# A chunked GLU after attention: down projections gathered in SBUF for plain chunks, and projection reads moved to the sync engine's queue

## The chip, the core and the metric

The kernel runs on one core of a Trainium2 chip. A core has a matrix engine (TensorE; PE in the profile, and PEld for its loading of weights), a vector engine (DVE), a scalar engine (ACT), a general engine (GpSimd, POOL) and a sync engine (SP), which issues transfers. Each works through its own list of instructions in order. Transfers (DMAs) are issued from the lists of SP, ACT or POOL and carried out by 16 DMA engines. The metric is the time on the device in microseconds.

## What is computed

The reference takes 2048 tokens of 576 numbers and runs one transformer layer in float32:

- a layer norm, a projection to queries, keys and values, attention with 32 heads of 18 numbers in which each token sees itself and 7 earlier tokens at a distance of 2, an output projection `wo`, and the sum with the input: `h = x + attention(layernorm(x))`
- a layer norm of `h`, and a gated linear unit with 4608 hidden columns: `h + (sigmoid(n @ w_gate) * (n @ w_up)) @ w_down`, where `n` is the normalised `h`.

The result, 2048 x 576 numbers, goes back to DRAM.

## The kernel before

**Tiles.** The tokens are four blocks of 512, numbered 0 to 3: even and odd tokens, first and second half. The hidden columns are 36 chunks of 128. Every matmul operand is split into a high part in TensorE's float32r form and a low part, the remainder (`split`, line 103: one ACT copy and one DVE subtraction), and a product is three matmuls: high by high, low by high, high by low.

**Stages.** After a first part (queries, keys, values for all blocks, the attention of block 0), a list of work items runs, lines 877 and 878: 14 *plain* chunks (`std`, function `single`) of block 0, then 22 *paired* chunks (`pair`) of blocks 0 and 1, then 14 plain chunks of block 1, and 36 paired chunks of blocks 2 and 3. A paired chunk computes gate and up products of two blocks with seven products in place of eight. So there are two plain stages, and they run a single block's products each.

**Weights.** At item `c` the loop (line 1003) splits the weights of item `c + 1` (`weights`, line 509) and issues the load of item `c + 2` (`load_gu`, line 501, on SP's queue): a tile `wg` of 128 x 1856 numbers with gate, up and down columns, in two buffers. A load waits until the weights two items earlier are split, and the last of those splits waits for a matmul, since the tile `w4` has one buffer.

**Down projection.** The hidden tiles of two chunks make one unit of down projection, `down_units` (line 643). It goes through four groups of 128 tokens; each takes 12 matmuls into a PSUM tile `dp` (two buffers), and ACT copies the result to a tile `stage` in SBUF (line 668; the pool `st`, line 494, has two buffers of it). After the fourth group, POOL issues a DMA that adds `stage` to an accumulator in DRAM, `hacc` of the block (line 672). After the last unit of a block, `hacc` is copied to the output. In the last stage most pairs of chunks go another way (`down_seven`), and four chunks at the end add on DVE to a tile `tail` (line 670).

**Background.** Between the products a generator does other work in small steps (`bg_step`; eight steps in a plain chunk): under the first plain and paired chunks, the rest of the attention of block 1, its output projection and layer norm (`proj_scr`, line 721) and the operands of the paired stage; later the attention of blocks 2 and 3, and under the second plain stage their projections and the operands for the last stage. `proj_scr` first reads, on POOL's queue, four tiles `oj` of attention output from DRAM, four tiles `hj` of the input, and the split weights `wow` (line 727 and line 758), then waits some steps, and then takes four token groups through `proj_j`: transposes of `oj`, matmuls with `wo`, addition to `hj`, layer norm, transposes. Each `hj` is written out by POOL (lines 742 and 745). After the projections a `stage` tile is set to zero by POOL (line 833), and ACT's queue writes it to DRAM as the start of sums for the last stage.

**Order.** The program is written out by hand, item by item, but a planner orders each engine's list: an instruction is placed when its inputs and buffers are ready in the planner's own model of time, and by priority (`tc.high_priority`) among those that are ready. On the chip each list is then kept in that order.

Of the kernel before, what the change touches and what calls it, by code (L numbers as in the profile page):

```python
# [29 lines left out]
NF = F // P  # L30
NS = 4
# [3 lines left out]
DX = D + DR  # L35
# [8 lines left out]
BLOCKS = [(0, 0), (0, 1), (1, 0), (1, 1)]  # L44
# [3 lines left out]
DH2 = D // 2  # L48
# [5 lines left out]
HC = 700  # L54
NSTD = 14
NPL = 4
# [4 lines left out]
def kernel(ctx, tc, x, wqkv, wo, wmlp, out):  # L61
    nc = tc.nc
    dve, act, pool, pe, sp = nc.vector, nc.scalar, nc.gpsimd, nc.tensor, nc.sync
# [11 lines left out]
    xv = x.rearrange("(h p j e) d -> e h p j d", e=2, h=2, j=NS)  # L75
    ov = out.rearrange("(h p j e) d -> e h p j d", e=2, h=2, j=NS)
# [21 lines left out]
    def f32(ap):  # L98
        return ap.bitcast(F32)
# [125 lines left out]
            live = [gn for gn in live if next(gn, END) is not END]  # L225


    def proj_j(bank, oj, hj, wos, th, tl, xn_tile, put, order=(0, 1)):
        pv = tr_main(bank(), oj)
        with tc.high_priority(HI):  # L230
            split(th[:, 0:4], tl, pv)
        yield
        pv = tr_rest(bank(), oj)
        with tc.high_priority(HI):
            split_rest(th[:, 4], pv)
        yield
        for i in order:
            ps = bank()
            tok_major(ps, DH2, th, tl, slice(0, P), *wos[i])
            hs = hj[:, i * DH2:(i + 1) * DH2]  # L240
            with tc.high_priority(HI):
                dve.tensor_tensor(hs, hs, ps[:, :DH2], ALU.add)
            yield
        xn = xn_tile()
        with tc.high_priority(HI):
            ln_j(hj, xn, False)
# [122 lines left out]
    o = None  # L369
# [63 lines left out]
    h = load_x(0)  # L433
# [10 lines left out]
    def front():  # L444
        ar = tok_tile((P, 5, TB))
        oT = th_tile(), tl_tile()
        gens = []
        for j in range(NS):
            js = slice(j * P, (j + 1) * P)

            def put(pv, cs, js=js):
                act.activation(ar[:, cs, js], pv, AF.Copy)

            gens.append(proj_j(any_bank, o[:, j], h[:, j], wos, oT[0][:, :, js], oT[1][:, :, js],
                               lambda j=j: o[:, j], put, (1, 0)))
# [181 lines left out]
        between(6)  # L637

    tails = {}
    segs = [0] * 4  # L640
    NSEG = NF // 2

    def down_units(seg, b, t):
        e, hf = BLOCKS[b]
        left = NSEG - 1 - segs[b]
        segs[b] += 1
        add = b < 2 or left > 1
        if add:
            hs = st.tile([P, NS, D], F32, name="stage")
        else:  # L650
            hs = tails[b]
        for j in range(NS):
            js = slice(j * P, (j + 1) * P)
            ps = gp.tile([P, 2, 512], F32, bufs=2, name="dp")
            k = 0
            n = 3 * len(seg) - 1
            for hid, d in seg:
                hh, hl = hid[t]
                for a, m in ((hh, 0), (hl, 0), (hh, 1)):
                    for i in range(2):  # L660
                        pe.matmul(ps[:, i, :DH2], a[:, js], d[:, m, i * DH2:(i + 1) * DH2],  # L661
                                  start=k == 0, stop=k == n)
                    k += 1
            hv = hs[:, j].rearrange("p (i n) -> p i n", i=2) if add else \
                hs[:, :, j // 2, (j % 2) * DH2:(j % 2 + 1) * DH2]
            with tc.high_priority(HC):
                if add:
                    act.activation(hv, ps[:, :, :DH2], AF.Copy)  # L668
                else:
                    dve.tensor_tensor(hv, hv, ps[:, :, :DH2], ALU.add)  # L670
            if add and j == NS - 1:
                pool.dma_start(hacc[b], hs, accum_op=ALU.add, max_dma_last_dim=8 * D)  # L672
                if left == 0:
                    pool.dma_start(ov[e, hf], hacc[b])
            elif not add and left == 0:
                sp.dma_start(ov[e, hf][:, j].rearrange("p (i n) -> p i n", i=2), hv)
            yield

# [39 lines left out]
            sp.dma_start(f32(ww[a]), wscr[1][:, a])  # L718
        return tuple(ww)

    def proj_scr(pj, b, raw, wos, wait, at=0):
        e, hf = BLOCKS[b]
        th, tl = th_tile(), tl_tile()

        def load(shape, name, src):
            t = pj.tile([P, shape], F32, bufs=NS, name=name)
            pool.dma_start(t, src)
            return t

        def tile_j(j, oj, hj):  # L730
            js = slice(j * P, (j + 1) * P)
            xj = []

            def put(pv, cs):
                if raw is None and not xj:
                    xj.append(pj.tile([P, 5, P], F32, bufs=2, name="xj"))
                act.activation(xj[0][:, cs] if raw is None else raw[:, cs, js], pv, AF.Copy)

            yield from proj_j(bg_bank, oj, hj, wos,
                              th[:, :, js], tl[:, :, js], lambda: oj, put, (1, 0))  # L740
            if b < 2:
                pool.dma_start(hacc[b][:, j], hj)
            else:
                rows = slice(0, 7, 6) if b == 2 else slice(2, 5, 2)
                pool.dma_start(hsev[:, j // 2, rows, j % 2],
                               hj.rearrange("p (i n) -> p i n", i=2))
            if raw is None:
                act.dma_start(xscr[b][:, :, js], xj[0])

        ojs, hjs = [], []  # L750
        for j in range(NS):
            ojs.append(load(DX, "oj", oscr[b][:, j]))
            yield
        for j in range(NS):
            hjs.append(load(D, "hj", xv[e, hf][:, j]))
            if wos[0] is None and j == 0:
                ww = pj.tile([P, 2, 5, DH2], F32R, name="wow")
                pool.dma_start(f32(ww), wscr[0])
                wos[0] = ww[:, 0], ww[:, 1]
            yield  # L760
        for _ in range(wait):
            yield
        while c < at:
            yield
        live = [tile_j(j, ojs[j], hjs[j]) for j in range(NS)]
        for _ in range(5):
            for gn in live:
                next(gn)
                yield
        for gn in live:  # L770
            yield from gn
        if raw is not None:
            act.dma_start(xscr[b][:, 0:2], raw[:, 0:2])

    def operands(pp, p, Xn, names, own):
        def load(t):
# [21 lines left out]
    def under_first():  # L798
        wos = [None, wos_early()]
        for _ in ag:  # L800
            yield ATT
        at_stk.close()
        a1 = xt.tile([P, 5, TB], F32, tag="th", bufs=3, name="ar")
        with sb_pool("pj", "right") as pj:
            yield from proj_scr(pj, 1, a1, wos, 4, 6)
        with sb_pool("pp", "right") as pp:
            yield from operands(pp, 0, X, ("s2", "s3", "s1", "a11", "s4"), a1)

# [4 lines left out]
    def under_rest(last_x):  # L813
# [13 lines left out]
            wos[1] = wos_early()  # L827
        with sb_pool("pj2", "right") as pj:
            a0 = xt.tile([P, 5, TB], F32, tag="th", bufs=3, name="ar")
            yield from proj_scr(pj, 2, a0, wos, 4)  # L830
            yield from proj_scr(pj, 3, None, wos, 0)
        z = st.tile([P, NS, D], F32, name="stage")
        pool.memset(z, 0.0)
        for u in range(2):
# [168 lines left out]
    for c, (kind, p, f) in enumerate(items):  # L1003
# [37 lines left out]
        else:  # L1041
# [14 lines left out]
            if f < NF - NPL:  # L1056
                if f % 2:
                    if f == 1:
                        queue.append(lag(LAG))
                    queue.append(seven())  # L1060
                    for b in blocks:
                        segs[b] += 1
                continue
            d = M[f]
        seg.append((hid, d))
        if len(seg) == 2:
            if by_seven and not tails:
                tails.update({2: None, 3: None})
# [48 lines left out]
```

## Time and profile before

| | us |
|---|---|
| median of 3 runs | 1668.56 (1667.79 to 1675.57) |
| the profiled execution | 1668.82 |
| its span, first to last instruction | 1667.0 |
| PE busy | 1579.7 (95%) |
| DVE busy | 1248.2 (75%) |
| ACT busy | 897.9 (54%) |
| POOL busy | 215.5 (13%) |

The stages in the profile, by the sigmoids of the plain chunks: the first plain stage runs from about 260 to 427 us, the paired chunks of blocks 0 and 1 follow until about 815, the second plain stage until about 1022, and the rest is the paired stage of blocks 2 and 3. "Busy" of PE counts pipelined matmuls, so it says when PE was not idle, not how fast it ran; the granted clock beside it says that. A wait is written "engine line tile <- engine line tile": who stood idle, and whose end let it go on.

### The profile page before, as it was taken

To read this page: it belongs to the slowest core of one execution; us is meant where nothing else is said; L and a number is where in the kernel's file an instruction comes from. 1 tells how busy PE (TensorE), PEld (TensorE's weight loads), DVE (VectorE), ACT (ScalarE), POOL (GpSimd) and SP (SyncE) were. 2 spreads that over 40 slices of the span, in tenths; PEclk is the share of its full clock that TensorE was granted. 3 is DMA by queue.
4 is the path that set the end of the run, shared out by engine and by line. 5 is a ranking of instruction groups with operands and counts; after the bars stand their busy time and mean duration, and the time that the engine had idled before them with its cause. 6 is when DMAs were issued, how large, how long until landed. Compare 5 with 4: busy or idle time off the path is not lost.

```text
span 1667.0 us, 22497 instructions
## 1 busy us (share of the span) xinstructions
PE 1579.7 (95%) x8532; PEld 1396.4 (84%) x8532; DVE 1248.2 (75%) x1954; ACT 897.9 (54%) x1583; POOL 215.5 (13%) x266
## 2 busy tenths in 40 slices
PE   7899877899999999999998988999999999999998
PEld 6799776788788888888897877788888888888887
DVE  7999999447799999999454446677776777667755
ACT  5422224426555656655434244677766777667761
POOL 2000010210000100000211200122122121221210
PEclk9999988999999999999999999999999999999999
DMA  7446534737557576575956366589888898888983
GB/s 252 158 162 229 213 143 165 233 112 236 144 151 184 149 178 169 131 190 145 290 156 191 103 203 151 148 164 192 173 174 172 166 190 173 174 171 171 189 172 109
DMA packets 81341, 290.82 MB, mean 174 GB/s; under 512 B 8560, under 2 KB 17008, under 8 KB 80208
## 3 DMA queue, kind: packets, MB, share of 16 engines
q0 software_dynamic: 33616, 133.31, 40.3%
q1 hardware_dynamic: 36416, 132.33, 24.5%
q10 hardware_dynamic: 11200, 23.73, 3.8%
q8 instruction: 67, 1.10, 0.3%
q14 instruction: 42, 0.34, 0.1%
HBM read 147.19 MB, written 144.51 MB: 175 GB/s over the span
## 4 chain that ended last, share of the span: by engine, by line
PE 72%; DVE 12%; DMA 9%; ACT 3%; issue 2%; POOL 0%; SPq 0%; ACTq 0%; DVEq 0%; POOLq 0%
PE b L543 37%; PE dp L661 12%; PE dp L694 11%; PE b L550 7%; DMA wg<-in_wmlp_dram 6%; PE acc L150 2%; DVE pr L198 2%; DVE pr L172 1%; DVE lg L175 1%; PE b L150 1%; PE bgp L150 1%; DVE pr L203 1%; DVE w L105 1%; DVE tl L105 1%; DMA h<-stage 1%
## 5 line engine op out<-in xcount | busy, mean ns | idle before, releaser
L543 PE MATMUL b<-tl,w 128*128 128x512 f32 x1728 | 446.5, 399 | 17.1 <-DVE w L105 7.7
L543 PEld LDWEIGHTS b<-tl,w 128*128 128x128 f32 x1728 | 315.4, 190 | 78.2 <-DVE w L105 8.4
L543 PE MATMUL b<-th,w 128*128 128x512 f32 x1380 | 361.1, 397 | 6.0 <-DVE s L563 3.0
L543 PEld LDWEIGHTS b<-th,w 128*128 128x128 f32 x1380 | 252.5, 189 | 60.3 <-DVE s L625 4.6
L105 DVE TENSOR_TENSOR w<-wg,w 128x384 fp32r<-128x384 f32 (+2 forms) x200 | 129.0, 649 | 107.3 <-ACT w L104 107.0
L104 ACT ACTIVATE w<-wg 128x384 fp32r<-128x384 f32 (+2 forms) x200 | 117.9, 595 | 115.4 <-DMA wg<-in_wmlp_dram 72.1
L550 PE MATMUL b<-th,w 128*128 128x512 f32 x576 | 178.8, 392 | 0.0
L703 POOL DMA_DIRECT2D h<-ev x128 | 110.4, 863 | 459.6 <-ACT ev L700 444.7
L700 ACT ACTIVATE ev<-dp 128x576 f32<-128x576 f32 x224 | 145.0, 647 | 33.3 <-PE dp L694 30.5
L150 PE MATMUL acc<-qw,th 128*128 128x432 f32 x512 | 156.0, 365 | 0.0
L105 DVE TENSOR_TENSOR w<-tw,w 128x512 fp32r<-128x512 f32 x116 | 79.6, 686 | 72.8 <-ACT w L104 72.1
L668 ACT ACTIVATE stage<-dp 128x576 f32<-128x576 f32 x144 | 92.5, 645 | 70.8 <-PE dp L661 69.5
L661 PE MATMUL dp<-d,h1h 128*128 128x288 f32 x640 | 122.6, 302 | 7.6 <-ACT h1h L104 6.7
L550 PEld LDWEIGHTS b<-th,w 128*128 128x128 f32 x576 | 109.1, 189 | 23.1
L661 PE MATMUL dp<-d,h0h 128*128 128x288 f32 x640 | 121.4, 300 | 2.0 <-ACT stage L668 2.0
L104 ACT ACTIVATE w<-tw 128x512 fp32r<-128x512 f32 x116 | 73.2, 631 | 83.5 <-PE b L543 78.5
L661 PEld LDWEIGHTS dp<-d,h1h 128*128 128x128 f32 x640 | 101.3, 194 | 11.3 <-ACT h1h L104 7.2
L661 PEld LDWEIGHTS dp<-d,h0h 128*128 128x128 f32 x640 | 101.4, 193 | 5.7 <-ACT stage L668 2.3
L150 PEld LDWEIGHTS acc<-qw,th 128*128 128x128 f32 x512 | 98.3, 192 | 4.6 <-ACT th L104 0.3
L672 POOL DMA_DIRECT2D h<-stage x36 | 43.5, 1208 | 440.4 <-ACT stage L668 409.1
L150 PE MATMUL acc<-qw,tl 128*128 128x432 f32 x256 | 93.4, 365 | 0.0
L172 DVE TENSOR_TENSOR pr<-kw,q 128x1152 f32<-128x1152 f32 x64 | 85.2, 1354 | 4.7 <-DMA kw<-k 4.1
(272 smaller groups left out, 2890.6 us busy)
## 6 DMA issues: line engine op xcount, KB each, us to landing
h<-ev POOLq DMA_DIRECT2D x96, 576.0 KB, 6.9
wg<-in_wmlp_dram SPq DMA_DIRECT2D x48, 928.0 KB, 5.9
h<-stage POOLq DMA_DIRECT2D x36, 1152.0 KB, 11.5
wg<-in_wmlp_dram SPq DMA_DIRECT2D x36, 640.0 KB, 4.7
kw<-k SPq DMA_DIRECT2D x16, 792.0 KB, 4.2
vw<-v SPq DMA_DIRECT2D x16, 792.0 KB, 4.8
wd<-in_wmlp_dram SPq DMA_DIRECT2D x18, 576.0 KB, 7.0
h<-ev POOLq DMA_DIRECT2D x32, 288.0 KB, 6.2
```

The costliest lines, as they stand in the source:

```text
L104: act.activation(hi, src, AF.Copy)
L105: splits.append(dve.tensor_tensor(lo, src, f32(hi), ALU.subtract))
L150: pe.matmul(ps[:, :n], a[:, c, js], m[:, c], start=k == 0, stop=False)
L172: dve.tensor_tensor(pr[:, i], kw[:, j:j + W], q[:, j].unsqueeze(1).broadcast_to([P, W, CG]), ALU.mult)
L543: pe.matmul(ps, wt[:, a, k0 + c], xx[:, m + c], start=first and k == 0, stop=k == 5, skip_group_check=True)
L550: pe.matmul(ps, wt[:, a, k0], xx[:, 4], start=False, stop=a == 1, skip_group_check=True)
L661: pe.matmul(ps[:, i, :DH2], a[:, js], d[:, m, i * DH2:(i + 1) * DH2], start=k == 0, stop=k == n)
L668: act.activation(hv, ps[:, :, :DH2], AF.Copy)
L672: pool.dma_start(hacc[b], hs, accum_op=ALU.add, max_dma_last_dim=8 * D)
L694: pe.matmul(ps[:, i, :DH2], a[x][:, js], m[y], start=k in (0, 1, 3) and q == 0, stop=q == 2, skip_group_check=True)
L700: act.activation(hs[:, k % 2], ps[:, :, :DH2], AF.Copy)
L703: pool.dma_start(hsev[:, u, k0:k + 1], hs[:, :k + 1 - k0], accum_op=ALU.add, max_dma_last_dim=8 * D)
```

## The change

Three things are changed, and one function is split up.

1. **Down projection of plain chunks.** `down_units` becomes a tile of matmuls (`down_tile`), an eviction (`add_tile`) and an accumulating DMA (`add_dram`), from which three functions are put together. For plain chunks, `down_std` takes one `stage` tile for all 7 units of a block: the first unit is copied to it by ACT, the six others are added to it by DVE, and one accumulating DMA is sent after the seventh. For paired chunks of blocks 0 and 1, `down_units` is as before; for the end of the last stage, `down_tail` is as before.
2. **Reads of the background projections.** `oj`, `hj` and `wow` are read on SP's queue. Two steps of the background are between two reads of `oj`; the `hj` tiles and `wow` are read during the first steps of the token groups. The reads for block 3 are issued as the token groups of block 2 end. The waiting steps go; the projection of block 1 starts its reads at item 5, where its token groups had waited for item 6.
3. **Write-out of `hj`.** POOL's DMA is issued when the layer norm is done and the first transpose's result is to be copied, not at the end of the token group.

```diff
-    def down_units(seg, b, t):
...
+    def add_tile(hv, ps, copy):
+        with tc.high_priority(HC):
+            if copy:
+                act.activation(hv, ps, AF.Copy)
+            else:
+                dve.tensor_tensor(hv, hv, ps, ALU.add)
...
+    def add_dram(b, hs):
+        pool.dma_start(hacc[b], hs, accum_op=ALU.add, max_dma_last_dim=8 * D)
+        segs[b] += 1
+        if segs[b] == 1 + (NF - NSTD) // 2:
+            e, hf = BLOCKS[b]
+            pool.dma_start(ov[e, hf], hacc[b])
...
+    def down_std(seg, b, n):
+        if n == 0:
+            tails[b] = st.tile([P, NS, D], F32, name="stage")
+        hs = tails[b]
+        for j in range(NS):
+            add_tile(halved(hs, j), down_tile(seg, b, j), n == 0)
+            if j == NS - 1 and n == NSTD // 2 - 1:
+                add_dram(b, hs)
+            yield
...
+    def load_j(pj, b, j, i):
+        e, hf = BLOCKS[b]
+        t = pj.tile([P, D if i else DX], F32, bufs=NS, name="hj" if i else "oj")
+        sp.dma_start(t, (xv[e, hf] if i else oscr[b])[:, j])
+        return t
...
             def put(pv, cs):
-                if raw is None and not xj:
-                    xj.append(pj.tile([P, 5, P], F32, bufs=2, name="xj"))
+                if cs.start == 0:
+                    if b < 2:
+                        pool.dma_start(hacc[b][:, j], t[1])
...
-        ojs, hjs = [], []
-        for j in range(NS):
-            ojs.append(load(DX, "oj", oscr[b][:, j]))
-            yield
-        for j in range(NS):
-            hjs.append(load(D, "hj", xv[e, hf][:, j]))
...
-        for _ in range(wait):
-            yield
-        while c < at:
-            yield
...
+        todo = []
+        if ins is None:
+            ins = []
+            for j in range(NS):
+                ins.append([load_j(pj, b, j, 0), None])
+                yield
+                yield
+            todo = [0, 1, None, 2, 3]
+        live = [tile_j(t, j) for j, t in enumerate(ins)]
+        n = 0
         for _ in range(5):
             for gn in live:
+                if todo and n % 2 == 0:
+                    j = todo.pop(0)
+                    if j is not None:
+                        ins[j][1] = load_j(pj, b, j, 1)
+                    elif wos[0] is None:
+                        ww = pj.tile([P, 2, 5, DH2], F32R, name="wow")
+                        sp.dma_start(f32(ww), wscr[0])
+                        wos[0] = ww[:, 0], ww[:, 1]
+                n += 1
                 next(gn)
                 yield
-        for gn in live:
+        nxt = []
+        for j, gn in enumerate(live):
             yield from gn
+            if after is not None:
+                nxt.append([load_j(pj, after, j, i) for i in range(2)])
...
-            yield from proj_scr(pj, 1, a1, wos, 4, 6)
+            while c < 5:
+                yield
+            yield from proj_scr(pj, 1, a1, wos)
...
-            yield from proj_scr(pj, 2, a0, wos, 4)
-            yield from proj_scr(pj, 3, None, wos, 0)
+            ins = yield from proj_scr(pj, 2, a0, wos, after=3)
+            yield from proj_scr(pj, 3, None, wos, ins)
...
             for b in blocks:
-                queue.append(down_units(seg, b, b % 2))
+                queue.append(down_std(seg, b, f // 2) if kind == "std" else
+                             down_tail(seg, b, f == NF - 1) if by_seven else down_units(seg, b))
```

More of the change, by code (lines that the diff above doesn't have):

```diff
@@ L225, in run, with proj_j @@
             live = [gn for gn in live if next(gn, END) is not END]
-    def proj_j(bank, oj, hj, wos, th, tl, xn_tile, put, order=(0, 1)):
+    def proj_j(bank, t, wos, th, tl, xn_tile, put, order=(0, 1)):
+        oj = t[0]
         pv = tr_main(bank(), oj)
@@ L239, in proj_j @@
             tok_major(ps, DH2, th, tl, slice(0, P), *wos[i])
-            hs = hj[:, i * DH2:(i + 1) * DH2]
+            hs = t[1][:, i * DH2:(i + 1) * DH2]
             with tc.high_priority(HI):
@@ L245, in proj_j @@
         with tc.high_priority(HI):
-            ln_j(hj, xn, False)
+            ln_j(t[1], xn, False)
         yield
@@ L452, in put @@
                 act.activation(ar[:, cs, js], pv, AF.Copy)
-            gens.append(proj_j(any_bank, o[:, j], h[:, j], wos, oT[0][:, :, js], oT[1][:, :, js],
+            gens.append(proj_j(any_bank, (o[:, j], h[:, j]), wos, oT[0][:, :, js], oT[1][:, :, js],
                                lambda j=j: o[:, j], put, (1, 0)))
@@ L639 @@
     tails = {}
-    segs = [0] * 4
-    NSEG = NF // 2
-    def down_units(seg, b, t):
-        e, hf = BLOCKS[b]
[L645 to L651, printed above, removed]
-        for j in range(NS):
[L653 to L675, printed above, removed]
@@ new lines, with down_tile @@
+    segs = [0] * 2
+    def down_tile(seg, t, j):
+        js = slice(j * P, (j + 1) * P)
+        ps = gp.tile([P, 2, 512], F32, bufs=2, name="dp")
+        k = 0
+        n = 3 * len(seg) - 1
+        for hid, d in seg:
+            hh, hl = hid[t]
+            for a, m in ((hh, 0), (hl, 0), (hh, 1)):
+                for i in range(2):
+                    pe.matmul(ps[:, i, :DH2], a[:, js], d[:, m, i * DH2:(i + 1) * DH2],
+                              start=k == 0, stop=k == n)
+                k += 1
+        return ps[:, :, :DH2]
@@ new lines, in add_tile, with halved @@
+    def add_tile(hv, ps, copy):
[4 more added lines that the diff above has]
+                dve.tensor_tensor(hv, hv, ps, ALU.add)
+    def halved(hs, j):
+        return hs[:, j].rearrange("p (i n) -> p i n", i=2)
+    def add_dram(b, hs):
[4 more added lines that the diff above has]
+            pool.dma_start(ov[e, hf], hacc[b])
@@ new lines, in down_units @@
+    def down_units(seg, b):
+        hs = st.tile([P, NS, D], F32, name="stage")
+        for j in range(NS):
+            add_tile(halved(hs, j), down_tile(seg, b, j), True)
+            if j == NS - 1:
+                add_dram(b, hs)
[7 more added lines that the diff above has]
+            if j == NS - 1 and n == NSTD // 2 - 1:
+                add_dram(b, hs)
+            yield
@@ L676, in down_units, with down_tail @@
+    def down_tail(seg, b, end):
+        e, hf = BLOCKS[b]
+        hs = tails[b]
+        for j in range(NS):
+            hv = hs[:, :, j // 2, (j % 2) * DH2:(j % 2 + 1) * DH2]
+            add_tile(hv, down_tile(seg, b - 2, j), False)
+            if end:
                 sp.dma_start(ov[e, hf][:, j].rearrange("p (i n) -> p i n", i=2), hv)
@@ L719, in wos_early, with proj_scr, tile_j @@
         return tuple(ww)
-    def proj_scr(pj, b, raw, wos, wait, at=0):
+    def load_j(pj, b, j, i):
[3 more added lines that the diff above has]
+        return t
+    def proj_scr(pj, b, raw, wos, ins=None, after=None):
         e, hf = BLOCKS[b]
         th, tl = th_tile(), tl_tile()
[L725 to L730, printed above, removed]
+        def tile_j(t, j):
             js = slice(j * P, (j + 1) * P)
@@ L734, in put @@
             def put(pv, cs):
-                if raw is None and not xj:
-                    xj.append(pj.tile([P, 5, P], F32, bufs=2, name="xj"))
[L737 to L746, printed above, removed]
+                if cs.start == 0:
+                    if b < 2:
+                        pool.dma_start(hacc[b][:, j], t[1])
+                    else:
+                        rows = slice(0, 7, 6) if b == 2 else slice(2, 5, 2)
+                        pool.dma_start(hsev[:, j // 2, rows, j % 2],
+                                       t[1].rearrange("p (i n) -> p i n", i=2))
+                    if raw is None:
+                        xj.append(pj.tile([P, 5, P], F32, bufs=2, name="xj"))
@@ L747, in tile_j @@
+                act.activation(xj[0][:, cs] if raw is None else raw[:, cs, js], pv, AF.Copy)
+            yield from proj_j(bg_bank, t, wos, th[:, :, js], tl[:, :, js], lambda: t[0], put, (1, 0))
             if raw is None:
                 act.dma_start(xscr[b][:, :, js], xj[0])
-        ojs, hjs = [], []
-        for j in range(NS):
-            ojs.append(load(DX, "oj", oscr[b][:, j]))
-            yield
-        for j in range(NS):
-            hjs.append(load(D, "hj", xv[e, hf][:, j]))
[L756 to L759, printed above, removed]
-            yield
@@ L761, in proj_scr @@
-        for _ in range(wait):
-            yield
-        while c < at:
-            yield
-        live = [tile_j(j, ojs[j], hjs[j]) for j in range(NS)]
+        todo = []
+        if ins is None:
+            ins = []
+            for j in range(NS):
+                ins.append([load_j(pj, b, j, 0), None])
[4 more added lines that the diff above has]
+        n = 0
         for _ in range(5):
             for gn in live:
+                if todo and n % 2 == 0:
[7 more added lines that the diff above has]
+                n += 1
@@ L768, in proj_scr @@
                 next(gn)
                 yield
-        for gn in live:
+        nxt = []
+        for j, gn in enumerate(live):
             yield from gn
+            if after is not None:
+                nxt.append([load_j(pj, after, j, i) for i in range(2)])
         if raw is not None:
             act.dma_start(xscr[b][:, 0:2], raw[:, 0:2])
+        return nxt
     def operands(pp, p, Xn, names, own):
@@ L804, in under_first @@
         with sb_pool("pj", "right") as pj:
-            yield from proj_scr(pj, 1, a1, wos, 4, 6)
+            while c < 5:
+                yield
+            yield from proj_scr(pj, 1, a1, wos)
         with sb_pool("pp", "right") as pp:
@@ L1060 @@
                     queue.append(seven())
-                    for b in blocks:
-                        segs[b] += 1
                 continue
@@ L1066 @@
         if len(seg) == 2:
-            if by_seven and not tails:
-                tails.update({2: None, 3: None})
+            if by_seven and f == NF - NPL + 1:
                 queue.append(load_tails())
             for b in blocks:
-                queue.append(down_units(seg, b, b % 2))
+                queue.append(down_std(seg, b, f // 2) if kind == "std" else
+                             down_tail(seg, b, f == NF - 1) if by_seven else down_units(seg, b))
             seg = []
```

## The prediction, made before the changed kernel was run

> **What bounds the kernel now.** I read the span first, then the busy time by stage, then what PE waited for in the stages where it isn't full, and last the chain of waits and the timeline round those waits. The rows of the stages give span, busy time of PE, PEld, DVE, ACT and POOL (with instruction counts), granted clock, DMA share and GB/s.
>
> ```profile
> span 1667.0 us, 22497 instructions
> ```
> ```profile
> 260.00:430.00 170.00, 157.56 (x843) 138.31 (x844) 103.77 (x170) 75.97 (x136) 19.55 (x26) 0.95 0.59 178
> 430.00:820.00 390.00, 390.00 (x2142) 345.14 (x2142) 366.04 (x494) 230.45 (x373) 37.63 (x40) 1.00 0.65 170
> 820.00:1046.00 226.00, 201.94 (x1145) 178.46 (x1143) 108.01 (x204) 92.89 (x174) 30.11 (x37) 0.96 0.62 170
> ```
>
> From 430 to 820 us (paired chunks) PE has no idle time at a clock of 1.00: nothing can be won there. The two stages of plain chunks, 260 to 430 (block 0) and 820 to 1046 (block 1), are different: PE idles 170 - 157.56 = 12.4 us in the first and 226 - 201.94 = 24.1 us in the second, 36.5 us together. The change touches these two stages and little else, so 36.5 us, and what the clock loses after each stop, is the most that it can win. What PE waited for there, in total, times and longest us, first 255 to 435, then 815 to 1050:
>
> ```profile
> PE bgp L143 <- DVE tl L105: 4.4, 1, 4.4
> PE b L543 <- DVE s L563: 3.0, 1, 3.0
> PE b L139 <- ACT ar L737: 2.1, 1, 2.1
> ```
> ```profile
> PE dp L661 <- ACT h1h L104: 6.7, 2, 3.8
> PE bgp L143 <- DVE tl L105: 3.5, 1, 3.5
> PE b L139 <- ACT xj L737: 3.4, 2, 2.8
> PE dp L661 <- ACT stage L668: 2.9, 2, 2.0
> PE b L543 <- ACT s L624: 2.8, 1, 2.8
> PE b L139 <- DVE tl L105: 2.6, 1, 2.6
> ```
>
> These are single stops on evictions by ACT and DVE, and those engines are half idle. So the question is what held ACT. In the same windows:
>
> ```profile
> ACT w L104 <- DMA wg<-in_wmlp_dram: 23.5, 7, 6.6
> ```
> ```profile
> ACT w L104 <- DMA wg<-in_wmlp_dram: 48.1, 12, 6.4
> ```
>
> ACT runs in order. It stands at the first split of the next chunk's weights until the GLU weights (`wg`) have landed, 71.6 us in all, and the evictions queued behind that split are what PE waits for. Time from issue to landing of `wg` in the first stage, then one case in detail (chain of waits; timeline):
>
> ```profile
> DMA to landing us min/median/max: 4.5/5.0/9.4
> ```
> ```profile
> 305.95 8.39 DMA wg<-in_wmlp_dram
> 318.43 9.41 DMA wg<-in_wmlp_dram
> ...
> 359.69 9.00 DMA wg<-in_wmlp_dram
> ...
> 904.49 8.51 DMA wg<-in_wmlp_dram
> ```
> ```profile
> 902.00 1.23 POOL L672 DMA_DIRECT2D h<-stage  x1 [9.76 <-ACT stage L668]
> ...
> 913.02 0.74 ACT L104 ACTIVATE w<-wg 128x640 fp32r<-128x640 f32 x1 [5.70 <-DMA wg<-in_wmlp_dram]
> ```
>
> Undisturbed, the load takes 4.5 to 5 us. The accumulating DMA of the down projection (`h<-stage`) started at 902.00; the load issued at 904.49 beside it took 8.51, ACT stood for 5.70, and PE for the 3.5 of the row above. That is the mechanism: a late landing of some 3.5 us reappears on PE almost one for one.
>
> **The change, part by part.** First the bytes. Issue rows (count, KB each, median us to landing) and queue rows (packets, MB, share of 16 engines):
>
> ```profile
> h<-stage POOLq DMA_DIRECT2D x36, 1152.0 KB, 11.5
> ```
> ```profile
> q0 software_dynamic: 33616, 133.31, 40.3%
> q1 hardware_dynamic: 36416, 132.33, 24.5%
> ```
>
> Each plain stage has 7 pairs of chunks; now only the last of each sends an accumulation, so 12 of the 36 go. At q0's rate, 133.31 MB in 40.3% of 1667 us = 198 GB/s, one (1.18 MB) takes 6.0 us of all 16 engines, 36 us per stage: the DMA share falls from 0.59 x 170 = 100 us to 64, and from 0.62 x 226 = 140 us to 104. No DMA of this size stands between a weight load and its landing any more, except where the reads of the projections are.
>
> Second, evictions. 6 pairs x 4 tiles x 2 blocks = 48 move from an ACT copy to a DVE addition. Duration rows (ns, min/median/max) of the copy and of the same 128x576 addition in the tail:
>
> ```profile
> L668 ACT ACTIVATE stage<-dp x144: 628/651/658, 280.8 to 1034.8; 128x576 f32<-128x576 f32 x144
> ```
> ```profile
> L670 DVE TENSOR_TENSOR tail<-tail,dp x16: 747/754/756, 1635.6 to 1663.2; 128x576 f32<-128x576 f32 x16
> ```
>
> ACT loses 48 x 0.651 = 31 us, DVE gains 48 x 0.754 = 36 us, 18 per stage: 122 of 170 and 126 of 226, still far from full. The `dp` tile has two buffers and about two fillings per chunk of some 10 us, which is what hides the 0.10 us longer eviction. If that cover were gone at every one, 36 us would be lost; at none, nothing, and ACT, the blocked engine, has less to do. I take 1 us, near nothing, because DVE is free of attention in most of both stages.
>
> Third, the stage buffers. The zeroes for the seven-product sums are cleared in a stage tile, between down projections. Here the memset waited for an accumulation to leave the buffer, and ACT, whose queue sends the zeroes, behind it:
>
> ```profile
> 956.33 2.02 POOL L833 MEMSET stage<- 128x2304 f32 x1 [5.61 <-DMA h<-stage]
> ...
> 958.87 0.42 ACT L104 ACTIVATE w<-wg 128x256 fp32r<-128x256 f32 x1 [2.14 <-POOL stage L833]
> ```
>
> With the sums staying in one of the two buffers, the other has been free for a hundred us. So the wait goes, and with it most of the 3.4 us on `xj` and the 0.9 that is the smaller of the two stops on `stage`: 4.3 us, of which I take 4.
>
> Fourth, the reads for the background projections, now on SP's queue instead of POOL's, beside a weight load:
>
> ```profile
> wg<-in_wmlp_dram SPq DMA_DIRECT2D x48, 928.0 KB, 5.9
> ...
> oj<-o POOLq DMA_DIRECT2D x12, 320.0 KB, 7.7
> ...
> hj<-in_x_dram POOLq DMA_DIRECT2D x12, 288.0 KB, 10.6
> ...
> wow<-wo POOLq DMA_DIRECT2D x2, 1440.0 KB, 11.0
> ```
> ```profile
> 303.77 2.23 POOL L727 DMA_DIRECT2D oj<-o  x4 [5.45 <-DMA o<-kw]
> ```
>
> Per first block of a group 4 x 320 + 4 x 288 + 1440 = 3872 KB, 3.97 MB. At q1's rate (132.33 MB in 24.5% of 1667 us = 324 GB/s) that is 12.2 us, and a weight load of 928 KB 2.9. Nothing is read less; 26 issues move to SP. If they all stand ahead of the load that was issued at 305.95 and landed 8.39 us later at 314.3, that one lands at 303.8 + 12.2 + 2.9 = 318.9, 4.6 us later; if they lie between loads, the burst is gone. So the stop of 4.4 us at 330 (the load of 318.43) is worth from -4.6 to +4.4 here. I take +3: that load stood beside an accumulation which goes in any case, and the backlog would be over by then. The write-outs of `hj` are issued two steps earlier on POOL, and 16 waiting or loading steps of the background go; both have slack, since nothing on PE waits for them: 0.
>
> By the Trainium skill (DMA: Bandwidth & Descriptors, "Issuing engines are not separate DMA queues") all queues end on the same 16 engines, so moving reads from POOL to SP wins no bandwidth. This trace can't show the moved reads; by the page this term would be 0 and the sum 3 us less.
>
> The sum, taken from the stops: 330 us: 3. The 2.1 us at 371 us (load of 359.69, slow for a still running accumulation): 2. The 3.0 us at 427 us: its load shared the engines with an accumulation and with window reads that stay: 1.5. The 2.6 and 3.5 us round 906 and 915: both loads beside accumulations, 6.1, and the clock lost behind them:
>
> ```profile
> 910.00:920.00 10.00, 6.30 (x26) 5.24 (x25) 4.49 (x9) 4.12 (x10) 0.00 (x0) 0.75 0.40 127
> ```
>
> 10 x 0.25 = 2.5 us more; of 8.6 I take 8. The zeroes: 4. The 2.8 us on `s` at the start of the last stage: half, 1.5, as its loads lay beside the sixth accumulation. The 6.7 us on `h1h` come from operands of the next stage on ACT and DVE: 0; the 2.0 us at 825 lie beside an accumulation of paired chunks and reads, which stay: 0. Together 3 + 2 + 1.5 + 8 + 4 + 1.5 = 20, less 1 for the additions: 19 us. The profiled execution took 1668.82 us (span and 1.8 us round it), 0.26 over the median of 1668.56: 1668.56 - 19 = **1649.5 us**. Its own range: the terms at their best (4.4 + 2.1 + 3.0 + 8.6 + 4.3 + 2.8, the 2.0 at 825, and some 7 for clock lost behind the other stops: 0.05 x 170 + 0.04 x 226 = 17.5 us in both stages) give 34 us, 1634; at their worse 12 us, 1656.
>
> **Rivals.** *The reads bunch in front of the weights.* The yields between the reads only set the order of emission; the reads of the trace went out in a row (2.23 us for four) as soon as their data was there. On SP's queue they would then stand ahead of a weight load instead of sharing the engines with it. For it: 3.97 MB must pass in either case. Against it: SP itself waits for buffers between loads, which spaces them. Then the 330 us term is -4.6, the 906/915 term 0 (there the second group's reads meet the loads), the rest stays: -4.6 + 2 + 1.5 + 4 + 1.5 - 1 = 3.4 us, 1665. That is no measurable change. The Trainium skill has it as a rule (the same page, "Queues, rings and completion order"): queues take turns packet by packet, but one queue's ring starts in order. The trace agrees only so far that a load beside POOL's traffic took 9 us instead of 5.
>
> *SP stands at a read* (the slower side). SP's queue is in order. A read placed ahead of a weight load whose own data comes later than the planner believed holds that load. It happens in this trace with window loads:
>
> ```profile
> SPq L165 <- DMA o<-kw: 75.0, 8, 13.0
> ```
> ```profile
> 296.58 35.97 SPq L503 DMA_DIRECT2D wg<-in_wmlp_dram  x4
> ```
> ```profile
> 794.92 0.33 SPq L503 DMA_DIRECT2D wg<-in_wmlp_dram  x1
> ...
> 812.73 0.54 POOL L758 DMA_DIRECT2D wow<-wo  x1 [3.82 <-DMA o<-kw]
> ```
>
> If the first `oj` (ready at 303.77) stood ahead of the load issued at 296.58, that one is 7.2 us late, and nine issues of 0.33 us make 10.2. If `wow` (ready at 812.73) stood ahead of the load of 794.92, 17.8. At one for one 28.0 us against 19 won: +9, 1678. It decides when both happen; with one of them the kernel is still no slower. Against it: attention ends on DVE shortly ahead of both, and the weight loads are ready early, so a planner has little reason to put the read first.
>
> **How the numbers follow.** About 0.5%, 8.3 us, is what a measurement here can tell from no change: faster means below 1660.2, slower above 1676.9. Forecast (1641 to 1656) 0.53; all terms at their best (below 1641) 0.12; bunched reads (1657 to 1668) 0.23, of which 0.03 lies below 1660.2; SP standing at a read (1670 and up) 0.12. Faster 0.53 + 0.12 + 0.03 = 0.68, within 0.20, slower 0.12. The range 1633 to 1668 leaves out the slow case and a little below, under 2 in 10.
>
> **What would show it.** Right: 24 accumulations from `stage`; DMA share near 0.38 and 0.46 in the two stages; ACT's wait for `wg` below a third of 71.6 us; landings of `wg` back at 5 us from 340 to 400 and 890 to 980; no wait of the memset; the last stage as long as before. Wrong: landings over 8 us at the reads (bunching), SP waiting on `o<-kw` or on the projections' tiles with a weight load next (SP stands), or PE waiting on `dp` for DVE in more than a few places (the additions cost more than 1 us).

## The result, and the profile after

| | before | after |
|---|---|---|
| median (us) | 1668.17 | 1645.18 (1643.16 to 1655.36, 4 runs) |
| ratio to before | | 0.9864, 95% interval 0.9814 to 0.9914 |
| the profiled execution | 1668.82 | 1647.17 |
| its span | 1667.0 | 1645.4 |

The kernel became faster, by 23 us where 19.0 were forecast (1649.5 us); the interval reaches from 14 to 31 us. Where it was won can be read from the sigmoids of the plain chunks. The first one of the second plain stage comes at 803.9 us of the span in place of 815.3, and the last one of that stage at 993.5 in place of 1015.5; what comes behind it takes as long as before (651.9 us after, 651.5 before). So about half was won up to the second plain stage and half in it. The stages of the kernel after (span, busy PE, PEld, DVE, ACT, POOL, clock, DMA share, GB/s), to be held against 157.56 of 170 and the DMA share of 0.59 in the first row before:

```profile
260.00:430.00 170.00, 166.60 (x903) 146.86 (x904) 125.37 (x199) 69.63 (x123) 6.52 (x11) 0.96 0.41 146
820.00:1046.00 226.00, 209.16 (x1175) 184.44 (x1175) 137.22 (x251) 88.21 (x162) 18.29 (x23) 0.96 0.47 146
```

The row of the accumulating DMA after, and what PE waited for in the two plain stages after, first 255 to 435 us, then 800 to 1050 us (who, for whom, total, times, longest):

```profile
h<-stage POOLq DMA_DIRECT2D x24, 1152.0 KB, 11.5
```
```profile
PE b L544 <- DVE w L105: 7.6, 1, 7.6
PE b L139 <- DVE tl L105: 3.4, 1, 3.4
```
```profile
PE bgp L143 <- DVE tl L105: 8.5, 1, 8.5
PE b L544 <- DVE r L977: 3.4, 1, 3.4
PE bgp L150 <- DVE hj L243: 3.3, 1, 3.3
PE b L139 <- ACT ar L769: 1.4, 1, 1.4
```

The first row is the wait of the first plain chunk for the split of its weights; it ends at 260 us. The kernel before has the same stop, which ends at 261 us, and the change does not touch it. The prediction's list of the first stage left it out, and with it a small stop at 320 us:

```profile
PE b L543 <- DVE w L105: 7.7, 1, 7.7
PE b L139 <- DVE tl L105: 1.6, 1, 1.6
```

Most of the stops quoted in the prediction are gone, also some that it had counted on to stay. But a stop of 8.5 us is new, and two of 3.3 and 3.4 us in the second stage are larger or in another place. What lies behind the 8.5 us, on SP's queue and on ACT and PE (timeline), with the time that the load of 811.48 took:

```profile
801.98 0.33 SPq L504 DMA_DIRECT2D wg<-in_wmlp_dram  x1
802.36 2.13 SPq L748 DMA_DIRECT2D oj<-o  x4
804.54 1.36 SPq L748 DMA_DIRECT2D hj<-in_x_dram  x2
805.94 0.66 SPq L793 DMA_DIRECT2D wow<-wo  x1
811.48 0.33 SPq L504 DMA_DIRECT2D wg<-in_wmlp_dram  x1
```
```profile
DMA to landing us min/median/max: 18.9/18.9/18.9
```
```profile
814.43 1.21 POOL L668 DMA_DIRECT2D h<-stage  x1 [10.96 <-ACT stage L660]
...
830.36 0.74 ACT L104 ACTIVATE w<-wg 128x640 fp32r<-128x640 f32 x1 [11.64 <-DMA wg<-in_wmlp_dram]
...
833.44 0.48 PE L143 MATMUL bgp<-ident,oj 128*128 128x128 f32 x1 [8.48 <-DVE tl L105]
```

Seven reads stand between two weight loads in SP's list: they are not spread between the loads, they are bunched. The load behind them landed after 18.9 us, ACT stood 11.6 us at its split, and PE 8.5. Accumulations began at 802.04 and 814.43 us, so this load met both of them too; an experiment below keeps them and moves the reads. The stop of 3.3 us has another chain, on POOL:

```profile
861.15 2.03 POOL L867 MEMSET stage<- 128x2304 f32 x1 [10.02 <-DMA h<-stage]
...
863.64 0.63 ACT L104 ACTIVATE h1h<-s 128x512 fp32r<-128x512 f32 x1 [7.54 <-POOL stage L867]
...
864.51 0.58 DVE L134 TENSOR_SCALAR oj<-hj,mv,rstd 128x576 f32<-128x576 f32 x1 [5.43 <-POOL rstd L126]
...
865.73 0.40 PE L150 MATMUL bgp<-wow,th 128*128 128x288 f32 x1 [3.28 <-DVE hj L243]
```

The planner put the clearing of the zeroes 95 us earlier (861 for 956 us), at a place where the stage buffer was still being sent; POOL waited 10 us, and the layer norm's step on POOL (`rstd`) and ACT's list waited behind it.

### The profile page after: what moved, and what is told of

Read it like the earlier page. It is cut to its first block, busy times and chain, and to the rows that moved or that the text cites. A ratio compares the mean times of both kernels' runs of the same rounds, so it can differ in the third digit from the quotient of the medians.

```text
span 1645.4 us, 22460 instructions
## 1 busy us (share of the span) xinstructions
PE 1573.6 (96%) x8532; PEld 1392.6 (85%) x8532; DVE 1279.6 (78%) x2002; ACT 873.6 (53%) x1535; POOL 185.2 (11%) x228
## 4 chain that ended last, share of the span: by engine, by line
PE 62%; issue 15%; DVE 10%; DMA 6%; POOL 4%; ACT 2%; SPq 0%; POOLq 0%; DVEq 0%; ACTq 0%
PE b L544 31%; PE dp L652 14%; PE b L551 6%; PE dp L718 6%; POOL h L727 3%; DMA wg<-in_wmlp_dram 3%; PE acc L150 2%; DVE pr L198 2%; DVE pr L172 1%; DVE lg L175 1%; PE b L150 1%; PE bgp L150 1%; DVE pr L203 1%; DMA h<-stage 1%; DVE pr L205 1%
## 5 line engine op out<-in xcount | busy, mean ns | idle before, releaser
L551 PE MATMUL b<-th,w 128*128 128x512 f32 x576 | 178.2, 391 | 0.0
L104 ACT ACTIVATE w<-wg 128x384 fp32r<-128x384 f32 (+2 forms) x200 | 118.1, 596 | 108.7 <-DMA wg<-in_wmlp_dram 45.1
L361 ACT ACTIVATE ev<-acc 128x432 f32<-128x432 f32 x64 | 33.3, 527 | 100.9 <-PE acc L153 97.5
L198 DVE TENSOR_TENSOR pr<-vw,lg 128x1152 f32<-128x1152 f32 x64 | 85.2, 1353 | 0.9
## 6 DMA issues: line engine op xcount, KB each, us to landing
h<-stage POOLq DMA_DIRECT2D x24, 1152.0 KB, 11.5
```

What stands on the lines that cost most here:

```text
L104: act.activation(hi, src, AF.Copy)
L198: dve.tensor_tensor(pr[:, i].rearrange("p w (h d) -> p w h d", d=DH), vw[:, j:j + W].rearrange("p w (h d) -> p w h d", d=DH), lg[:, j].uns ...
L361: act.activation(ev[:, :, j], ps[:, :NQ].rearrange("p (t c) -> p t c", t=3), AF.Copy)
L551: pe.matmul(ps, wt[:, a, k0], xx[:, 4], start=False, stop=a == 1, skip_group_check=True)
```

## Experiments

Two theories were open. *A*: the accumulating transfers made the weight loads late, and taking them away made the gain. Its rivals: *B*, the reads on SP's queue made it; *C*, it was the relief of ACT and of the stage buffers, not the traffic. All times below are medians, and each ratio is to the kernel before on the same chip.

### Gathering alone, and the reads alone

The first kernel has `down_std` and `add_dram` of the change, with `proj_scr` as before. The second has the change, with accumulations as before (the count at which `hacc` is copied out goes with them and is not shown):

```diff
-                queue.append(down_std(seg, b, f // 2) if kind == "std" else
-                             down_tail(seg, b, f == NF - 1) if by_seven else down_units(seg, b))
+                queue.append(down_tail(seg, b, f == NF - 1) if by_seven else down_units(seg, b))
```

> Only the down projections of the plain chunks are gathered in SBUF; the reads of the projections stay on POOL's queue, as before. Theory A (the accumulating transfers delayed the weight loads): nearly all of the gain is here, 1640 to 1650 us, ACT's wait for wg in the two plain stages below 30 us of 71.6, and no stop over 5 us in the second stage (the changed kernel has one of 8.48 us at the reads). Rival B (the reads on SP's queue made the gain): 1660 us or more.

> Only the reads move to SP's queue; every pair of plain chunks sends its accumulating transfer as before. Theory A: no gain, 1664 to 1678 us, with the 36 accumulations back, landings of wg at 8 to 10 us back and a stop of some 8 us at the reads of the second plain stage. Rival B: 1645 to 1655 us.

Gathering alone: 1636.24 us, 0.9804 (0.9776 to 0.9833). That is 9 us better than the whole change, and beyond what was expected. ACT's wait for `wg` in its two plain stages (255 to 440, 790 to 1050 us):

```profile
ACT w L104 <- DMA wg<-in_wmlp_dram: 15.9, 8, 4.4
```
```profile
ACT w L104 <- DMA wg<-in_wmlp_dram: 29.0, 10, 7.9
```

That is 44.9 of 71.6 us, not the under 30 that was expected, yet no PE stop over 3.0 us is left but that of the first chunk at 262 us (7.4). The reads alone: 1649.80 us, 0.9892 (0.9858 to 0.9926). Theory A expected nothing there. Its profiled execution, the slowest of four (1657.06 us), shows a stop of bunched reads in the first stage (10.0 us) and only 1.0 us at the reads of the second, where some 8 us were expected. It is still 19 us faster, with all 36 accumulations. So A does not explain everything, and the two parts do not add up: 32 and 19 us alone, 23 together.

### Steps and queue apart

The reads alone contain two things: the queue, and the steps of the background (16 fewer, reads between steps, `hj` written out earlier). One kernel has the steps with the reads on POOL's queue, another the kernel before with only the queue exchanged (first the edit to the kernel with the reads alone, then the one to the kernel before):

```diff
-        sp.dma_start(t, (xv[e, hf] if i else oscr[b])[:, j])
+        pool.dma_start(t, (xv[e, hf] if i else oscr[b])[:, j])
```
```diff
-            pool.dma_start(t, src)
+            sp.dma_start(t, src)
```

(`wow` likewise in both.)

> The run with the reads alone (1649.8 us, accumulations as before) gained 19 us, against the forecast of none. Here it is the same kernel, but with the reads on POOL's queue again: the steps as changed (no waiting steps, reads between the steps, hj written out earlier, the start at item 5), the queue as before. Theory S (the new steps shift the units and loads of the second plain stage against each other): 1645 to 1655 us. Theory Q (SP's queue itself): 1662 to 1670 us.

> The kernel before with nothing but the queue of the reads changed, POOL's to SP's; its steps, waiting steps and write-outs stay. Theory S (the new steps make the gain of the reads alone): no gain, 1664 to 1676 us, with a stop of 5 us or more at the reads of the first plain stage. Theory Q (the queue makes it): 1645 to 1655 us.

Steps only: 1650.16 us, 0.9885 (0.9865 to 0.9906). Queue only: 1670.69 us, 1.0003 (0.9990 to 1.0015). So the queue alone is worth nothing, and the steps alone all of the 19 us. In the profiled executions they win it in the second plain stage: from its first to its last sigmoid it takes 184.8 us in place of 200.2, and the first plain stage 152.3 in place of 151.4. The queue alone is worth nothing in sum only: it makes a stop of 11.1 us at the reads of the first plain stage, which then takes 155.5 us, and the second takes 196.9. The Trainium skill says this of the queue (DMA: Bandwidth & Descriptors, "Issuing engines are not separate DMA queues"): who issues a transfer makes no bandwidth, as the same 16 engines carry it. This pair agrees.

ACT's wait for `wg` from 800 to 1055 us with the new steps alone, where before had 48.1 from 815 to 1050:

```profile
ACT w L104 <- DMA wg<-in_wmlp_dram: 19.8, 9, 6.3
```

The number of accumulations issued from 840 to 1040 us is the same in both (8). What differs is when weight loads are issued after them. For all loads issued from 840 to 1040 us, I took the time since the last accumulation began and the time to landing. Before, 5 of 13 loads came 1.2 to 3.8 us behind one, and took 6.8 to 9.2 us (four of them 8.5 or more); the two that were issued in the same instant took 5.3 and 5.6. With the new steps, 2 of 15 loads came 1.7 and 3.7 us behind one (10.7 and 8.2 us), and two that had fallen in that gap came 5.2 and 5.3 us behind (6.2 and 6.4). With the queue alone the pattern is that of before: 5 loads 1.1 to 3.5 us behind, 6.8 to 9.5 us. So the steps shift the loads against the accumulations. That a load in the gap is the one that suffers is a regularity of these traces; why the steps bring just this shift has not been shown.

### Gathering and steps, reads on POOL's queue

```diff
-        sp.dma_start(t, (xv[e, hf] if i else oscr[b])[:, j])
+        pool.dma_start(t, (xv[e, hf] if i else oscr[b])[:, j])
```

> The changed kernel with the reads on POOL's queue: gathering and the new steps, not the new queue. The changed kernel (1645.2 us) is 9 us behind the gathering alone (1636.2 us). If reads ahead of a weight load in SP's own list cost that, the stop of 8.48 us at 833 us goes below 4 us here and the time is 1634 to 1640 us. If the new steps cost it, once the accumulations are gone, the time stays at 1643 to 1648 us.

1636.35 us, 0.9801 (0.9776 to 0.9826): as good as gathering alone. So the steps bring nothing more once the accumulations are gone (most likely because both avoid the same collisions), and the queue costs 9 us there. The weight load that stands in the place of the one of 811.48 is issued at 812.01 us; accumulations begin at 802.58 and 814.96 us, much as beside that one, and the same reads pass. It took:

```profile
DMA to landing us min/median/max: 8.3/8.3/8.3
```

That is 8.3 us in place of 18.9, so it was the reads ahead of it on its own queue. The 8.5 us stop is gone; the PE waits of this kernel from 780 to 1050 us begin with:

```profile
PE bgp L150 <- DVE hj L243: 3.9, 1, 3.9
PE b L544 <- DVE r L977: 3.1, 1, 3.1
PE b L139 <- DVE tl L105: 1.0, 1, 1.0
```

### The reads kept behind a weight load

Each read on SP's queue is tied behind the weight load of its own chunk (`behind[0]` is the last load that `load_gu` issued, and `issue_after` keeps the read behind that instruction in the list; `wow` likewise):

```diff
-        sp.dma_start(t, (xv[e, hf] if i else oscr[b])[:, j])
+        with tc.issue_after(behind[0]):
+            sp.dma_start(t, (xv[e, hf] if i else oscr[b])[:, j])
```

> The changed kernel, but each read of the projections is kept behind the weight load of its own chunk in SP's list, so that the list alternates between loads and reads. If the reads standing ahead of a weight load cause the stops of 3.40 us (at 321 us) and 8.48 us (at 833 us) of the changed kernel, both fall below 2.5 us and the time to 1632 to 1640 us. If the bytes have to pass in any case, or the later reads only move the stop to the projections, 1642 to 1650 us.

1628.33 us, 0.9758 (0.9726 to 0.9789), 17 us better than the change as made. In the first stage no stop is left but that of the first chunk (7.6 us at 261 us). From 785 to 1050 us PE and ACT waited:

```profile
PE bgp L150 <- DVE hj L243: 3.6, 1, 3.6
PE b L547 <- DVE r L982: 3.1, 1, 3.1
```
```profile
ACT w L104 <- DMA wg<-in_wmlp_dram: 12.9, 9, 3.1
```

The same bytes pass, on the same queue. It is the order in the list that made the 8.5 us. This is the second rule named in the prediction (the same page of the Trainium skill, "Queues, rings and completion order": a ring starts its entries in order), and here the runs agree: 18.9 us for the load behind seven reads, 8.2 us for its counterpart behind four small ones (issued at 805.05 us), which stops PE no more.

### The traffic put back

To tell the traffic from the relief of ACT, the 12 transfers were put back without their evictions and stage buffers: 1024 KB each, from an operand tile that does not change in the stage, to a DRAM tile that nothing reads. The first of each block is a plain write, the other ten accumulate.

```diff
+        i = pool.tensor_tensor(tick, hs[:, NS - 1, D - 1:D], mhalf, ALU.mult)
+        with tc.issue_after(getattr(i, "ins", i)):
...
+                pool.dma_start(dummy[b], src, accum_op=ALU.add, max_dma_last_dim=8 * D)
```

A first version, on the kernel with the change, has neither the product nor `issue_after` and so was not tied to its place:

> The changed kernel, but each of the 12 pairs that no longer send an accumulation sends one of 1024 KB from a tile that doesn't change (the high and low halves of an operand) to a DRAM tile of its own, which nothing reads. The additions on DVE, the copies taken off ACT and the free stage buffer stay. Theory A (it is the traffic): the gain goes back by two thirds or more, 1660 to 1668 us, wg landings of 8 to 10 us again. Rival C (the relief of ACT and the free stage buffer made the gain): 1643 to 1650 us.

It took 1665.82 us, 0.9983 (0.9968 to 0.9998), but its transfers went out as soon as the operands were there, five of them from 259 to 302 us, with a stop of 16.3 us at 265 us. It says that such traffic costs time, not what it cost at its old place. The tied version, on top of the reads kept behind the loads:

> The kernel with the reads behind the weight loads (1628.3 us), and after each pair of plain chunks that sends no accumulation, POOL waits for its last eviction (a product of one column) and then sends an accumulation of 1024 KB from a tile that doesn't change to a DRAM tile that nothing reads: the traffic of before at its place, without its evictions on ACT and its use of the stage buffers. Theory A (the traffic delays the weight loads): weight loads that start 1 to 4 us behind such a transfer land after 8 to 10 us, and the time rises by 10 to 20 us, to 1638 to 1648. Rival C (relief of ACT): within 4 us of 1628.

1649.82 us, 0.9896 (0.9862 to 0.9929): 21.5 us more than the kernel without the traffic (1628.33). From first to last sigmoid the first plain stage takes 146.7 us in place of 138.9, the second 189.1 in place of 177.2. ACT's wait for `wg` (255 to 440, then 785 to 1050 us) is:

```profile
ACT w L104 <- DMA wg<-in_wmlp_dram: 24.4, 8, 4.4
```
```profile
ACT w L104 <- DMA wg<-in_wmlp_dram: 16.7, 10, 5.4
```

Without the traffic it was 8.4 and 12.9. So in the first stage the late loads come back; in the second they do so only in part, and what else the traffic holds there has not been taken apart. (Once, at 1012 us, ACT stood 5.9 us until a transfer had read its operand tile, which the next stage overwrites; PE lost 0.8 us or less by it.) One case from its first plain stage (timeline, then the time that this load took):

```profile
373.02 1.21 POOL L697 DMA_DIRECT2D dummy<-tl  x1
375.93 0.33 SPq L506 DMA_DIRECT2D wg<-in_wmlp_dram  x1
384.95 0.74 ACT L104 ACTIVATE w<-wg 128x640 fp32r<-128x640 f32 x1 [4.37 <-DMA wg<-in_wmlp_dram]
```
```profile
DMA to landing us min/median/max: 9.0/9.0/9.0
```

Theory A stands: with evictions on DVE and the stage buffer free, the traffic alone costs what A said, 10 to 20 us and a little more. Nothing speaks for C: with the traffic back the kernel takes as long as with the steps alone (1650.16 us), where evictions and stage buffers are those of before, though the reads lie on another queue there. With the steps of before, no run tells A from C.

### What the additions on DVE cost

```diff
                 dve.tensor_tensor(hv, hv, ps, ALU.add)
+                if again:
+                    dve.tensor_tensor(hv, hv, hv, ALU.max)
```

(`again` is set for plain chunks.)

> The kernel with the reads behind the weight loads (1628.3 us), with a second DVE instruction of the same 128x576 size (a maximum of the tile with itself) behind each of the 48 additions: 48 x 0.6 to 0.75 = 29 to 36 us more on DVE. If the additions lie beside PE's work (the prediction: 1 us for the 48), the time stays within 3 us, 1626 to 1632. If evictions on DVE hold PE, it takes a good part of the 29 to 36 us: 1638 us or more.

1631.15 us, 0.9778 (0.9745 to 0.9812), 2.8 us over the 1628.33 of the same kernel without them. The added instructions (DVE groups, busy us and mean ns):

```profile
L667 DVE TENSOR_TENSOR stage<-stage 128x576 f32<-128x576 f32 x48 | 36.1, 755 | 0.7
```

36.1 us of work more on DVE, behind every one of these additions, cost 2.8 us in the medians, which the runs do not tell from nothing, as they overlap (1627.0 to 1629.9 and 1627.7 to 1635.3). In the traces the first plain stage takes 138.9 us from first to last sigmoid in both kernels, the second 178.2 in place of 177.2. The additions are covered.

### The two stops that were left

On top of the reads kept behind the loads, the clearing of the zeroes is held behind the last write-out of `hj` on POOL (`behind[1]`):

```diff
-        pool.memset(z, 0.0)
+        with tc.issue_after(behind[1]):
+            pool.memset(z, 0.0)
```

> The kernel with the reads behind the weight loads (1628.3 us), and the clearing of the zeroes held behind the last write-out of hj on POOL. In that kernel and in the changed one the planner puts the clearing some 90 us earlier than before, where it waits 10 us for an accumulation of a paired chunk; ACT (8.5 us) and POOL's power for the layer norm stand behind it, and PE 3.57 us at 849 us. Theory: that stop goes, and the wait of POOL for a stage buffer falls below 1 us: 1622 to 1626 us. If that stop only uncovers another one beside it: 1627 to 1630 us.

1626.26 us, 0.9742 (0.9709 to 0.9776). The stop of 3.6 us went, but one of 2.8 us came in its place, on `xj` as before the change; the gain of 2 us is half of what the stop was, and the intervals of the two kernels overlap. Then, on top of it, the last accumulation of block 1 by token groups:

```diff
-            if j == NS - 1 and n == NSTD // 2 - 1:
+            if n == NSTD // 2 - 1 and b == 1:
+                pool.dma_start(hacc[b][:, j], hs[:, j], accum_op=ALU.add, max_dma_last_dim=8 * D)
...
+            elif j == NS - 1 and n == NSTD // 2 - 1:
                 add_dram(b, hs)
```

> As the run with the clearing held, and the last accumulation of block 1, 1152 KB after the fourth token group, goes out as four of 288 KB, one after each token group. In the changed kernel the first hidden tile of the last stage waits 3.4 us for that transfer to leave the stage buffer (its 9.3 us). Theory: the wait falls to 1 us or less, and the time by 2 to 4 us against the run with the clearing held. Rival: the hidden tile is held by something else that is due at the same time, and the time stays within 1 us of that run.

1621.81 us, 0.9722 (0.9694 to 0.9751), 4.5 us less in the medians, though single runs of the two overlap. The wait on `r` is gone; all that PE waited for from 785 to 1050 us:

```profile
PE b L139 <- ACT xj L779: 2.1, 1, 2.1
PE dp L655 <- ACT h1h L104: 0.7, 1, 0.7
PE dp L655 <- DVE h1l L105: 0.6, 1, 0.6
```

This kernel is 46 us below the one before and 23 below the change.

## Why the prediction was right, point by point

**The bound.** Right: the late weight loads hold ACT and through it PE, only in the plain stages, and the traffic put back at its place brings late loads back and costs 21.5 us. The loads land in 5 us again where the accumulations are gone (the gathering alone: 4.4 to 4.9 us from 319 to 397 us). With the whole change the sign that the prediction named came too; these are the loads of 340 to 400 and of 890 to 980 us, first after, then before:

```profile
DMA to landing us min/median/max: 4.5/4.6/5.0
DMA to landing us min/median/max: 4.5/4.6/5.7
```
```profile
DMA to landing us min/median/max: 4.5/6.9/9.0
DMA to landing us min/median/max: 4.5/8.8/9.6
```

**The terms at 371, 427 and 906 to 915 us.** Right in kind, a little small: the stops of 2.1, 3.0, 2.6 and 3.5 us are gone altogether. The 2.5 us of clock in the last term cannot be seen: the clock of that stage is 0.96 before and after.

**The 6.7 us on `h1h` and the 2.8 on `s`.** Wrong in the first: it was taken as 0, for work on operands. Neither is among the waits after. With the gathering alone 0.5 us of the `h1h` stops is left. That step failed because it looked at the last releaser only; ahead of these stops, at 1000 and 1022 us, ACT had stood 5.7 and 4.7 us for late loads as well (issued at 986 and 1004 us, landed after 6.9 and 6.8).

**The additions on DVE.** 1 us was taken of a possible 36; a second instruction behind each adds 2.8 us in the medians and 1 us in the two stages of the traces, so the term was near enough.

**The zeroes.** Wrong. The step said that the wait goes since one buffer has been free for a hundred us, worth 4 us. But the planner moved the clearing ahead, to a place where the buffer was not free yet, and there POOL waited 10.0 us in place of 5.6, ACT 7.5 in place of 2.1, and PE 3.3. Held behind the write-outs that stop went, with one of 2.8 us in its place.

**The reads.** The step that failed is the 0 at 825 us. The rival of bunched reads was what happened in both places, though not with the sizes given for it. At the first burst the load landed after 10.6 us and PE lost 3.4 (1.6 and 4.4 before, with accumulations beside the reads): 2.6 us were won there, near the 3 that were taken, and with the reads on POOL's queue 2.9 us are lost in place of 3.4. At the second burst, where nothing was taken, 2.0 us became 8.5. Together the moved reads cost 9 us against the same kernel with reads on POOL's queue; on the kernel before, the same move cost nothing in sum. So the sum came out near by luck, because two errors cancelled: the reads, taken at 3 us to the good, cost 9, and the gathering alone gave 32 us where the terms other than the reads came to 16. Of these 16 us too little, some 6 are the `h1h` stops; the rest has not been taken apart.

**The slower rival.** SP did stand at a read, but no weight load was late by it. In the first stage SP waited 6.7 us at the first `oj` for its data; the load behind the reads went out at 306.1 us, and at 306.0 before. In the second the load of 802 us went out ahead of the reads. Of the signs named, the 24 accumulations and the DMA shares came (0.41 and 0.47, forecast 0.38 and 0.46); ACT's wait did not fall to a third: it was 45.1 us in the two stages, of which the bunched reads hold 11.6 in one piece:

```profile
ACT w L104 <- DMA wg<-in_wmlp_dram: 16.7, 8, 5.2
```
```profile
ACT w L104 <- DMA wg<-in_wmlp_dram: 28.4, 9, 11.6
```

## What to carry to other kernels

When an in-order engine stops at a late load, look first at which large transfers were in flight beside it, and take bytes away before moving them between queues: the queue alone was worth nothing here, and in front of the loads it cost 9 us. Where a planner writes the lists, positions in the program do not spread transfers; an ordering edge behind the load that must not wait does (17 us here). Two changes that avoid the same collision do not add up, so each must be run alone before either is credited.

## What the runs showed of the hardware that was not expected

How late a weight load lands goes with when it is issued after an accumulating DMA of 1152 KB has begun. In the trace of before, of the loads issued from 255 to 1045 us, the 13 that came 1 to 4.5 us behind one took 9.0 us in the median (6.8 to 10.0). The 9 that came within 1 us took 5.0 to 5.9, apart from the one that also met the reads of the projections (10.5). The 28 with none begun for 8 us took 4.8 in the median, with a few up to 9.6. In the kernel with the traffic put back the medians are 8.8 (7 loads), 5.7 (15) and 4.9 us (29). The accumulation itself took 8.8 us with nothing beside it but the last 1.9 us of a weight load, nearly twice the time of a plain load of 928 KB; the row is from the kernel after:

```profile
435.22 1.25 POOL L668 DMA_DIRECT2D h<-stage  x1 [62.33 <-DVE stage L662]
```
```profile
DMA to landing us min/median/max: 8.8/8.8/8.8
```

So a load issued together with an accumulation lands about half way through it, and one issued two or three microseconds later lands when the accumulation does or a little before (11.5 us behind its start, in the median). Why is open; no run here takes the queues apart.
